# Linear attention ahead of two expert layers: the output products on 64x64 quadrants, k v in small PSUM tiles, the first k and v loaded first

## The chip, the cores and the metric

One Trainium2 chip, one of its cores. The metric is device time in microseconds (us); lower is better. Engines are named as in the profile: PE (TensorE matmul), PEld (TensorE weight load), DVE (VectorE), ACT (ScalarE), POOL (GpSimd), SP (SyncE, which issues most of the DMAs).

## What is computed

All data are fp32: q, k, v of 8 batches x 8 heads x 576 positions x 64. The change lies in the attention, the first of three stages.

```python
kv = np.einsum('bhsd,bhse->bhde', k, v)
out = np.einsum('bhsd,bhde->bhse', q, kv)
rms = np.sqrt(np.mean(out * out, axis=-1, keepdims=True) + 1e-06)
attn = out / rms * g_norm
x = attn.transpose(0, 2, 1, 3).reshape(4608, 512)
...
```

Behind it, x goes through two expert layers of 8 experts each (512 to 1024 to 512, with relu between). The first sends each token to the expert with the largest cosine logit, scaled by that expert's probability. The second gives every expert 576 tokens, by the order of all logits.

## The kernel before

**Attention (lines 267 to 351).** Each head's 64x64 matrix k v is made once and then multiplied with all of q. With the head's 64 columns go 8 more (E), the head's part of the gate logits, so a head's matrix is 64 x 72 (KW = 72). Batches are taken in pairs, four groups (gi = 0 to 3) of two batches; a group has two halves of four heads (hg). A half group is five units (u = 0 to 4): unit u is a transpose of q (`qa`, line 301: four PE transposes into a PSUM tile "tp" and one ACT copy to qT) and an output product (`qb`, line 313). Units 0 to 3 hold 2 of the 9 positions that a partition keeps, 128 rows of qT; unit 4 holds the last one, 64 rows. In all there are 40 units, 32 whole ones and 8 half ones (group 3 takes its two half units last).

`kv(m)` (line 267) makes the matrices of one batch's four heads, m = 0 to 15, in two steps. First 36 products of 64x64 by 64 columns add k v over the 9 positions in one PSUM tile (line 277), and ACT copies the result twice side by side into kvn (line 282). Two pumps later four products with `gex` (line 288) turn a head's matrix and append the gate's 8 columns; two copies of 64 partitions each (line 292, one by DVE, one by ACT) bring them to `kvx`. There each head has 2 x 72 columns: the upper 64 rows hold the matrix in the first 72, the lower 64 rows in the second 72, and the other two quarters are zero (memsets on POOL, line 261). So one product of 128 rows of qT by 144 columns gives the results of both positions, and half of its factors are zero.

`qb` makes 8 such products of 128x64 (line 333, 64 columns of output partitions for each of the two batches). Then come a copy of the 64 columns into the row tile x (line 340 or 342; DVE, or ACT where the unit's number in the group stands in EVAC, line 52), ACT's square (line 345), ACT's copy of the logits (line 347), and, one unit later on DVE, the sum of the squares (line 350).

**PSUM.** The pool has three kinds of tile with two buffers each: "mm" (two banks: output products, both steps of `kv`), "tp" (transposes) and "sm" (gate, slots and table of `group_end`). A buffer's next use waits until its last reader is done. The Tile framework also sets one engine's access to a PSUM tile behind another's.

**Order.** Every engine runs its instructions in the order of the program text. The loop of lines 894 to 929 takes the units in turn: unit n+2's transposes, unit n's output products, and then `pump()`, one step of every generator in `bg`: `kv` of the next half group (appended at units 1 and 2 of each half group; the last two at 0 and 1) and `group_end` of the group before (appended at a group's first unit). `group_end` (line 353) is norm, logits, expert choice, slots and table: some 30 small DVE instructions, some on ACT and POOL, three kinds of products on PE and the stores of x. Weight casts (`wcast`, ACT and DVE) stand at the units of CASTS, weight loads at those of LOADS.

**Loads (lines 130 to 163).** SP issues all q, k and v loads, 0.59 MB each. k and v have four buffers each, q six; load m+4 of k and v is issued when the products of m have been issued, and waits on SP's queue until these are done. The first in the queue are the expert embeddings, tau and g_norm (lines 154, 156, 158), then k and v of m = 0.

**Start (lines 851 to 878).** 44 transposes of the identity on PE; DVE's chain on the embeddings (`gate_weights`, lines 225 to 248, with one square root on ACT); the first step of kv(0) and kv(1); the gate's transposes on PE and their copies to `gex`; then the second steps of kv(0) and kv(1), and the units.

**Behind attention.** `group_end(3)` and the expert layers, from about 145 us on, fill the other 930 us. The diff touches none of it.

Of the kernel before, what the change touches and what calls it, by code (L numbers as in the profile page):

```python
# [7 lines left out]
F32 = mybir.dt.float32  # L8
# [3 lines left out]
AF = mybir.ActivationFunctionType  # L12
OP = mybir.AluOpType
AX = mybir.AxisListType
# [34 lines left out]

PEG = (4.5, 0.0)  # L50

EVAC = ((4, 8), (1, 2, 4, 5, 7, 8, 9), (1, 2, 4, 5, 7, 8, 9), tuple(range(10)))

CASTS = {25: 0, 26: 0, 28: 0, 32: 0, 34: 0, 36: 0}

# [16 lines left out]
def fused_kernel(ctx, tc, q, k, v, g_norm, emb, tau, w1, w2, wgate, v1, v2, out):  # L72
    nc = tc.nc
    V = nc.vector
    B, H, S, D = q.shape
# [18 lines left out]
    psum = pss.enter_context(tc.tile_pool(name="psum", bufs=2, space=PSUM))  # L94
# [9 lines left out]
    def mk(pool, shape, dtype, name, **kw):  # L104
        if pool is mp:
            pool = MP[name in MP0]
        return pool.tile(shape, dtype, name=name, **kw)
# [15 lines left out]
    ap = att.enter_context(tc.tile_pool(name="att", bufs=2, side="right"))  # L123
# [6 lines left out]
    def load_main(b, nm, hg):  # L130

        s = {"k": k, "v": v, "q": q}[nm]
        i = 4 * (b // 2) + 2 * hg + b % 2
        t = mk(ap, [128, 2, KR, D], F32, "qmain", bufs=6) if nm == "q" else KVL[nm, i % NL]
        nc.sync.dma_start(t.rearrange("p h r d -> p h (r d)"),
                          src(s, (b * H + 4 * hg) * S * D, [[KR * D, 128], [2 * S * D, 2], [1, KR * D]]))
        LD[nm, b, hg] = t


    def load_kv(m):  # L140
        for nm in "kv":
            load_main(m // 4 * 2 + m % 2, nm, m // 2 % 2)

    def load_q(ph):
        for j in range(2):
            load_main(ph // 2 * 2 + j, "q", ph % 2)
# [3 lines left out]
    for i in range(NL):  # L150
        for nm in "kv":
            KVL[nm, i] = mk(kvp, [128, 2, KR, D], F32, f"{nm}main{i}")
    em = mk(gp, [128, 1, XP], F32, "xt", bufs=2)[:E, 0, :HD]
    nc.sync.dma_start(em, emb)
    tau8 = con([E, 1], F32, "tau8")
# [1 line left out]
    gB = con([128, D], F32, "gB")  # L157
    nc.sync.dma_start(gB, src(g_norm, 0, [[0, 128], [1, D]]))
    for m in range(4):
        load_kv(m)  # L160
        if m % 2:
            load_q(m // 2)

# [87 lines left out]
    KW = D + E  # L251
# [4 lines left out]
    V.memset(run, 0.0)  # L256
    NKV = 4

    kvx = [mk(ap, [128, 2, 4, 2, KW], F32, f"kvx{i}", bufs=1) for i in range(NKV)]
    for t in kvx:  # L260
        nc.gpsimd.memset(t, 0.0)

    def kvh(b, h):
        hg, a, s = h // 4, h // 2 % 2, h % 2
        return kvx[b % NKV][:, a ^ s, 2 * s + hg]

    def kv(m):

        b, hg = m // 4 * 2 + m % 2, m // 2 % 2
        kvn = mk(ap, [128, 2, 2, D], F32, "kvn", bufs=2)  # L270
        p = mk(psum, [128, 2, 512], F32, "mm")
        kt, vt = LD["k", b, hg], LD["v", b, hg]
        for r in range(KR):
            for s in range(2):
                for a in range(2):
                    c = s ^ a
                    nc.tensor.matmul(p[64 * c:64 * c + 64, s, :D],
                                     vt[64 * s:64 * s + 64, a, r, :], kt[64 * s:64 * s + 64, a, r, :],
                                     start=(r == 0), stop=(r == KR - 1))
        if m + NL < 2 * B:  # L280
            load_kv(m + NL)
        nc.scalar.copy(kvn, p[:, :, None, :D].to_broadcast([128, 2, 2, D]))
        yield
        yield
        p = mk(psum, [128, 2, 512], F32, "mm")
        for s in range(2):
            for c in range(2):
                nc.tensor.matmul(p[:, c, s * KW:(s + 1) * KW], kvn[64 * c:64 * c + 64, s].rearrange("p u d -> p (u d)"),
                                 gex[64 * c:64 * c + 64, s, hg], start=True, stop=True)
        x = kvx[b % NKV]  # L290
        for r in range(2):
            (nc.scalar.copy if r else V.tensor_copy)(x[64 * r:64 * r + 64, :, hg:4:2, r],
                p[64 * r:64 * r + 64, :, :2 * KW].rearrange("p c (i w) -> p c i w", w=KW))
        yield

    GS = {}
# [16 lines left out]
    def qb(gi, u, hg, late, i):  # L313
        if u == 0 and hg == 0:
            GS[gi] = dict(s1=mk(gp, [128, TG * H], F32, "s1", bufs=2), lp=mk(gp, [128, TG * H, E], F32, "lp", bufs=2))
        if hg == 0:
            GS[gi]["x", u] = mk(gp, [128, 2, XP], F32, "xo", bufs=8) if u < 4 else mk(gp, [128, 1, XP], F32, "xt", bufs=2)
        G = GS[gi]
        qT = QT.pop((gi, u, hg))
        po = mk(psum, [128, 2, 512], F32, "mm")  # L320
        n = 8 if u < 4 else 4
        if u < 4:
            ov = po[:, :, :4 * KW].rearrange("p a (h r w) -> p a h r w", h=2, r=2)
        else:
            ov = po[:, :, :2 * KW].rearrange("p a (c w) -> p a c w", w=KW)
        for a in range(2):
            for s in range(2):
                for j in range(2):
                    kv_ = kvh(2 * gi + j, 4 * hg + 2 * a + s)
                    qt = qT[:, 2 * j + a, 64 * s:64 * s + 64]  # L330
                    if u == 4:
                        kv_, qt = kv_[:64, 0], qt[:64]
                    nc.tensor.matmul(ov[64 * j:64 * j + 64, a, s], qt, kv_, start=True, stop=True)  # L333
        o3 = po[:, :, :n // 2 * KW].rearrange("p a (c w) -> p a c w", w=KW)
        sq = mk(ap, [128, 8, D], F32, "sq")
        x = G["x", u]
        c0 = u * 16 + hg * n
        cp = nc.scalar.copy if i in EVAC[gi] else V.tensor_copy
        if u < 4:
            cp(x[:, :, hg * 4 * D:(hg + 1) * 4 * D].rearrange("p r (a c d) -> p a c r d", a=2, c=2), ov[:, :, :, :, 0:D])  # L340
        else:
            cp(x[:, 0, hg * 4 * D:(hg + 1) * 4 * D].rearrange("p (a c d) -> p a c d", a=2, c=2), ov[:, :, :, 0:D])
        if late is not None:
            late()
        nc.scalar.activation(sq[:, :n].rearrange("p (a c) d -> p a c d", a=2), o3[:, :, :, 0:D], AF.Square)

        nc.scalar.copy(G["lp"][:, c0:c0 + n].rearrange("p (a c) n -> p a c n", a=2), o3[:, :, :, D:KW])  # L347

        def later():
            V.tensor_reduce(G["s1"][:, c0:c0 + n], sq[:, :n], axis=AX.X, op=OP.add)  # L350
        return later

    def group_end(gi):
# [458 lines left out]
    def logits_w(e, c):  # L812
        N = WID[0, e][c]
        i = e - (E - ND)
        parts = [H7[0][:, :, 256 * c:256 * c + N]] if e == E - 1 else [h.bitcast(F32)[:, :, :N] for h in HT[0, e, c]]
        pl = mk(psum, [128, 512], F32, "sm")
        for kf in range(KF):
            g = kf % 4
            for x, p in enumerate(parts):
                nc.tensor.matmul(pl[32 * g:32 * g + 32, :N], W2G[0][:, i, kf - g:kf - g + 4, :].rearrange("p k e -> p (k e)"),  # L820
                                 p[:, kf, :], start=(kf < 4 and x == 0), stop=(kf >= 4 and x == len(parts) - 1),
                                 tile_position=(0, 32 * g))
        lgT = mk(mp, [128, C1 - 256], F32, "lgT")
        nc.scalar.copy(lgT[:, :N], pl[:, :N])
        return lambda: rows_l(e, c, lgT, 40)
# [45 lines left out]

    bg = []
    kv0, kv1 = kv(0), kv(1)
    next(kv0)
    next(kv1)
# [18 lines left out]
    for n, st in enumerate(steps):  # L894
        gi, u, hg = st
        i = n % 10
        ph, l = divmod(n, 5)
        l -= KVAT if ph + 2 < 2 * NG else 0
        if ph + 1 < 2 * NG and 0 <= l < 2:
            bg.append(kv(2 * ph + 2 + l))  # L900
        if n + 2 < len(steps):
            qa(*steps[n + 2])
        if n % 5 == 3 and ph + 3 < 2 * NG:
            load_q(ph + 3)
        late = qb(*st, late, i)
        if i == 0 and gi > 0:
            bg.append(group_end(gi - 1))
# [502 lines left out]
    a = logits_w(e6, 0)  # L1410
    xtiles(0, e7, 2, 3)
    a()
    b = logits_w(e6, 1)
# [77 lines left out]
    a = logits_w(e7, 1)  # L1491
# [232 lines left out]
    for e in range(1, E):  # L1724
        for g in range(2):
            for i in range(2):
                f = 2 * i + g
# [397 lines left out]
```

## Time and profile before

| | us |
|---|---|
| median of 3 runs (1075.4 to 1078.71) | 1076.03 |
| the profiled execution, its own time | 1077.35 |
| its span | 1075.6 |
| PE busy, share of the span | 1027.9, 96% |
| DVE, ACT, POOL busy | 727.3, 529.7, 298.1 |
| attention: first to last output product | 21.2 to 137.1 |

The span runs from the first to the last instruction on the device. Durations below are of the one profiled execution. "Idle before, releaser" is an engine's idle time ahead of an instruction and the instruction that ended it. A matmul's rows count records: one fp32 product is two matmul records and two weight loads, and a row of the timeline merges neighbours of the same kind.

### The profile page before, as it was taken

The numbers are of one execution on the slowest core, as the hardware profiler recorded it, in microseconds if no ns is written. First come the engines' busy times: TensorE is split into PE (matmuls) and PEld (weight loads), VectorE is DVE, ScalarE is ACT, GpSimd is POOL, SyncE is SP. The second block draws the span as 40 slices with busy tenths as digits, with TensorE's granted clock in tenths as the row PEclk, the third lists the DMA queues.
The fourth block names the chain that finished last, engine by engine and source line by source line (L and its number), as shares of the span: only waits on it lengthen the run. The fifth ranks groups of instructions, "written<-read, shape, count | busy, mean of one in ns | idle before, by whom it ended". The sixth has DMA issues, their size and how long they took to land. (4 is left out here: it accounts for less than half of the span.)

```text
span 1075.6 us, 21056 instructions
## 1 busy us (share of the span) xinstructions
PE 1027.9 (96%) x8497; PEld 937.0 (87%) x8497; DVE 727.3 (68%) x1440; ACT 529.7 (49%) x921; POOL 298.1 (28%) x396
## 2 busy tenths in 40 slices
PE   8998769899999999999999998999999999999998
PEld 7776669889999999999988987989889898989896
DVE  4466585376977778786756765677685959595860
ACT  2566633564444435363543322456565656555551
POOL 2022428261616051432400112222314131313211
PEclk8999989999999999999999999999999999999999
DMA  8999364544343535343311114435344343434311
GB/s 318 347 342 336 101 221 148 168 142 139 118 133 107 159 96 163 97 153 112 124 60 53 48 37 125 155 104 163 129 135 146 109 159 118 148 98 150 106 55 44
DMA packets 86040, 152.37 MB, mean 142 GB/s; under 512 B 6998, under 2 KB 39766, under 8 KB 85938
## 3 DMA queue, kind: packets, MB, share of 16 engines
q1 hardware_dynamic: 74450, 114.35, 32.5%
q0 software_dynamic: 10960, 36.10, 10.2%
q8 instruction: 67, 1.10, 0.4%
q10 hardware_dynamic: 528, 0.52, 0.2%
q14 instruction: 35, 0.29, 0.1%
HBM read 121.14 MB, written 29.82 MB: 140 GB/s over the span
## 5 line engine op out<-in xcount | busy, mean ns | idle before, releaser
L666 PE MATMUL mm<-xh,whi 128*128 128x256 f32 (+8 forms) x512 | 155.6, 304 | 9.8 <-ACT xh L636 6.6
L711 PE MATMUL mm<-hh,whi 128*128 128x256 f32 (+8 forms) x512 | 156.9, 306 | 1.5 <-ACT hh L683 1.5
L712 PE MATMUL mm<-hl,whi 128*128 128x256 f32 (+8 forms) x512 | 152.5, 298 | 1.1 <-DVE hl L1474 0.6
L667 PE MATMUL mm<-xl,whi 128*128 128x256 f32 (+8 forms) x512 | 152.8, 298 | 0.3 <-DVE xl L637 0.3
L668 PE MATMUL mm<-xh,wlo 128*128 128x256 f32 (+8 forms) x512 | 152.8, 298 | 0.0
L713 PE MATMUL mm<-hh,wlo 128*128 128x256 f32 (+8 forms) x512 | 152.2, 297 | 0.0
L808 DVE SCALAR_TENSOR_TENSOR rc<-xg,big 128x512 bf16<-128x512 f32 x128 | 111.1, 868 | 2.6
L666 PEld LDWEIGHTS mm<-xh,whi 128*128 128x128 f32 x512 | 97.9, 191 | 11.5 <-ACT xh L636 6.8
L548 DVE TENSOR_TENSOR wlo<-wraw,whi 128x1024 fp32r<-128x1024 f32 x72 | 90.8, 1263 | 24.4 <-ACT whi L542 23.9
L711 PEld LDWEIGHTS mm<-hh,whi 128*128 128x128 f32 x512 | 97.5, 190 | 3.5 <-ACT hh L683 1.8
L712 PEld LDWEIGHTS mm<-hl,whi 128*128 128x128 f32 x512 | 97.6, 191 | 1.5 <-DVE hl L1474 0.8
L667 PEld LDWEIGHTS mm<-xl,whi 128*128 128x128 f32 x512 | 97.8, 191 | 0.5 <-DVE xl L637 0.5
L668 PEld LDWEIGHTS mm<-xh,wlo 128*128 128x128 f32 x512 | 97.8, 191 | 0.0
L713 PEld LDWEIGHTS mm<-hh,wlo 128*128 128x128 f32 x512 | 97.4, 190 | 0.0
L720 ACT COPY yT<-mm 128x512 f32<-128x512 f32 (+8 forms) x31 | 19.9, 643 | 156.7 <-PE mm L713 156.7
L615 POOL DMA_INDIRECT xg<-xbuf,tabi x40 | 42.9, 1072 | 168.6 <-ACT sj L574 93.9
L2024 POOL DMA_INDIRECT out<-tm,ti x40 | 40.6, 1016 | 163.2 <-ACT tm L2022 143.6
L542 ACT CAST whi<-wraw 128x1024 fp32r<-128x1024 f32 x72 | 74.8, 1042 | 0.1
L683 ACT ACTIVATE hh<-mm 128x512 fp32r<-128x512 f32 (+7 forms) x56 | 36.8, 658 | 73.5 <-PE mm L668 70.2
L1767 DVE TENSOR_TENSOR wlo<-wraw,whi 128x1024 fp32r<-128x1024 f32 (+1 forms) x63 | 61.0, 986 | 11.6 <-ACT whi L1770 11.6
L333 PE MATMUL mm<-kvx,qT 128*64 128x144 f32 (+1 forms) x640 | 51.6, 297 | 12.1 <-ACT lp L347 6.4
L2034 POOL DMA_INDIRECT xg<-ybuf,tab x40 | 44.7, 1116 | 61.0 <-SPq L1559 25.6
(354 smaller groups left out, 2692.2 us busy)
## 6 DMA issues: line engine op xcount, KB each, us to landing
wraw<-in_moe_w SPq DMA_DIRECT2D x127, 512.0 KB, 3.5
kmain<-in_k SPq DMA_DIRECT2D x16, 576.0 KB, 6.6
vmain<-in_v SPq DMA_DIRECT2D x16, 576.0 KB, 13.5
qmain<-in_q SPq DMA_DIRECT2D x16, 576.0 KB, 12.0
ybuf<-yr SPq DMA_DIRECT2D x32, 260.0 KB, 2.2
xbuf<-xo POOLq DMA_DIRECT2D x12, 528.0 KB, 9.4
xg<-in_moe_w SPq DMA_DIRECT2D x16, 256.0 KB, 3.7
xbuf<-xo SPq DMA_DIRECT2D x4, 528.0 KB, 2.8
```

The source lines that it names most:

```text
L333: nc.tensor.matmul(ov[64 * j:64 * j + 64, a, s], qt, kv_, start=True, stop=True)
L542: nc.scalar.copy(hi, raw)
L548: eng.tensor_tensor(lo, raw, hi.bitcast(F32), op=OP.subtract)
L666: nc.tensor.matmul(o, a, xh[:, kd, :N], start=(kd == 0), stop=False)
L667: nc.tensor.matmul(o, a, xl[:, kd, :N], start=False, stop=False)
L668: nc.tensor.matmul(o, b, xh[:, kd, :N], start=False, stop=(kd == KD - 1))
L711: nc.tensor.matmul(o, a, hh[:, kf, :N], start=(kf == 0), stop=False)
L712: nc.tensor.matmul(o, a, hl[:, kf, :N], start=False, stop=False)
L713: nc.tensor.matmul(o, b, hh[:, kf, :N], start=False, stop=(kf == KF - 1))
L808: V.scalar_tensor_tensor(junk, raws[i], 1.0, wgB[:, x], op0=OP.mult, op1=OP.mult, accum_out=w2g[:, i // KF, i % KF, x:x + 1])
L1767: V.tensor_tensor(l, x, h.bitcast(F32), op=OP.subtract)
L2034: nc.gpsimd.indirect_dma_start(out=xg[:n, :YP], out_offset=None, in_=ybuf[:, :], in_offset=bass.IndirectOffsetOnAxis(ap=tab2[:n, e * SC + ...
```

## The change

The output products of a whole unit become 16 of 64x64 by 72 columns, each with the rows of one position (r) and the columns of one batch (j); the positions lie in separate PSUM banks. Half units keep their 8 products in another order. `kvx` loses its zero quarters and their memsets: all 128 rows hold each head's matrix, twice. The tiles of `kv` move from "mm" to "sm", two small tiles for each step, and their copies are cut by tile. The copies by ACT and DVE are handed out anew (EVAC). The loads of k and v of m = 0 are issued ahead of the embeddings, tau and g_norm.

```diff
--- before.py
+++ after.py
@@ -49,7 +49,7 @@
 
 PEG = (4.5, 0.0)
 
-EVAC = ((4, 8), (1, 2, 4, 5, 7, 8, 9), (1, 2, 4, 5, 7, 8, 9), tuple(range(10)))
+EVAC = ((4, 8), (1, 3, 5, 7, 9), (1, 3, 5, 7, 9), (1, 2, 3, 5, 6, 7, 8, 9))
 
 CASTS = {25: 0, 26: 0, 28: 0, 32: 0, 34: 0, 36: 0}
 
@@ -150,6 +150,7 @@
     for i in range(NL):
         for nm in "kv":
             KVL[nm, i] = mk(kvp, [128, 2, KR, D], F32, f"{nm}main{i}")
+    load_kv(0)
     em = mk(gp, [128, 1, XP], F32, "xt", bufs=2)[:E, 0, :HD]
     nc.sync.dma_start(em, emb)
     tau8 = con([E, 1], F32, "tau8")
@@ -157,7 +158,8 @@
     gB = con([128, D], F32, "gB")
     nc.sync.dma_start(gB, src(g_norm, 0, [[0, 128], [1, D]]))
     for m in range(4):
-        load_kv(m)
+        if m:
+            load_kv(m)
         if m % 2:
             load_q(m // 2)
 
@@ -256,9 +258,7 @@
     V.memset(run, 0.0)
     NKV = 4
 
-    kvx = [mk(ap, [128, 2, 4, 2, KW], F32, f"kvx{i}", bufs=1) for i in range(NKV)]
-    for t in kvx:
-        nc.gpsimd.memset(t, 0.0)
+    kvx = [mk(ap, [128, 2, 4, KW], F32, f"kvx{i}", bufs=1) for i in range(NKV)]
 
     def kvh(b, h):
         hg, a, s = h // 4, h // 2 % 2, h % 2
@@ -268,29 +268,29 @@
 
         b, hg = m // 4 * 2 + m % 2, m // 2 % 2
         kvn = mk(ap, [128, 2, 2, D], F32, "kvn", bufs=2)
-        p = mk(psum, [128, 2, 512], F32, "mm")
+        p = [mk(psum, [128, D], F32, "sm") for _ in range(2)]
         kt, vt = LD["k", b, hg], LD["v", b, hg]
         for r in range(KR):
             for s in range(2):
                 for a in range(2):
                     c = s ^ a
-                    nc.tensor.matmul(p[64 * c:64 * c + 64, s, :D],
+                    nc.tensor.matmul(p[s][64 * c:64 * c + 64],
                                      vt[64 * s:64 * s + 64, a, r, :], kt[64 * s:64 * s + 64, a, r, :],
                                      start=(r == 0), stop=(r == KR - 1))
         if m + NL < 2 * B:
             load_kv(m + NL)
-        nc.scalar.copy(kvn, p[:, :, None, :D].to_broadcast([128, 2, 2, D]))
-        yield
-        yield
-        p = mk(psum, [128, 2, 512], F32, "mm")
+        for s in range(2):
+            nc.scalar.copy(kvn[:, s], p[s][:, None, :].to_broadcast([128, 2, D]))
+        yield
+        yield
+        x = kvx[b % NKV]
+        p = [mk(psum, [128, 2, KW], F32, "sm") for _ in range(2)]
         for s in range(2):
             for c in range(2):
-                nc.tensor.matmul(p[:, c, s * KW:(s + 1) * KW], kvn[64 * c:64 * c + 64, s].rearrange("p u d -> p (u d)"),
+                nc.tensor.matmul(p[c][:, s], kvn[64 * c:64 * c + 64, s].rearrange("p u d -> p (u d)"),
                                  gex[64 * c:64 * c + 64, s, hg], start=True, stop=True)
-        x = kvx[b % NKV]
-        for r in range(2):
-            (nc.scalar.copy if r else V.tensor_copy)(x[64 * r:64 * r + 64, :, hg:4:2, r],
-                p[64 * r:64 * r + 64, :, :2 * KW].rearrange("p c (i w) -> p c i w", w=KW))
+        for c in range(2):
+            (nc.scalar.copy if c else V.tensor_copy)(x[:, c, hg:4:2], p[c])
         yield
 
     GS = {}
@@ -318,36 +318,28 @@
         G = GS[gi]
         qT = QT.pop((gi, u, hg))
         po = mk(psum, [128, 2, 512], F32, "mm")
-        n = 8 if u < 4 else 4
-        if u < 4:
-            ov = po[:, :, :4 * KW].rearrange("p a (h r w) -> p a h r w", h=2, r=2)
-        else:
-            ov = po[:, :, :2 * KW].rearrange("p a (c w) -> p a c w", w=KW)
-        for a in range(2):
-            for s in range(2):
-                for j in range(2):
-                    kv_ = kvh(2 * gi + j, 4 * hg + 2 * a + s)
-                    qt = qT[:, 2 * j + a, 64 * s:64 * s + 64]
-                    if u == 4:
-                        kv_, qt = kv_[:64, 0], qt[:64]
-                    nc.tensor.matmul(ov[64 * j:64 * j + 64, a, s], qt, kv_, start=True, stop=True)
-        o3 = po[:, :, :n // 2 * KW].rearrange("p a (c w) -> p a c w", w=KW)
+        m = 2 if u < 4 else 1
+        n = 4 * m
+        ov = po[:, :m, :4 * KW].rearrange("p r (c w) -> p r c w", w=KW)
+        for c in range(4):
+            for j in range(2):
+                for r in range(m):
+                    nc.tensor.matmul(ov[64 * j:64 * j + 64, r, c],
+                                     qT[64 * r:64 * r + 64, 2 * j + c // 2, c % 2 * 64:c % 2 * 64 + 64],
+                                     kvh(2 * gi + j, 4 * hg + c)[64 * r:64 * r + 64], start=True, stop=True)
         sq = mk(ap, [128, 8, D], F32, "sq")
         x = G["x", u]
         c0 = u * 16 + hg * n
         cp = nc.scalar.copy if i in EVAC[gi] else V.tensor_copy
-        if u < 4:
-            cp(x[:, :, hg * 4 * D:(hg + 1) * 4 * D].rearrange("p r (a c d) -> p a c r d", a=2, c=2), ov[:, :, :, :, 0:D])
-        else:
-            cp(x[:, 0, hg * 4 * D:(hg + 1) * 4 * D].rearrange("p (a c d) -> p a c d", a=2, c=2), ov[:, :, :, 0:D])
+        cp(x[:, :, hg * 4 * D:(hg + 1) * 4 * D].rearrange("p r (c d) -> p r c d", c=4), ov[:, :, :, 0:D])
         if late is not None:
             late()
-        nc.scalar.activation(sq[:, :n].rearrange("p (a c) d -> p a c d", a=2), o3[:, :, :, 0:D], AF.Square)
-
-        nc.scalar.copy(G["lp"][:, c0:c0 + n].rearrange("p (a c) n -> p a c n", a=2), o3[:, :, :, D:KW])
+        sqv = sq[:, :n].rearrange("p (r c) d -> p r c d", r=m)
+        nc.scalar.activation(sqv, ov[:, :, :, 0:D], AF.Square)
+        nc.scalar.copy(G["lp"][:, c0:c0 + n].rearrange("p (c r) n -> p r c n", r=m), ov[:, :, :, D:KW])
 
         def later():
-            V.tensor_reduce(G["s1"][:, c0:c0 + n], sq[:, :n], axis=AX.X, op=OP.add)
+            V.tensor_reduce(G["s1"][:, c0:c0 + n].rearrange("p (c r) -> p r c", r=m), sqv, axis=AX.X, op=OP.add)
         return later
 
     def group_end(gi):
```

## Rows read from the trace of the kernel before

**Rows 1.** Windows: length, then busy us (instructions) by engine, PEclk, DMA share, GB/s.

```profile
21.21:48.30 27.09, 25.84 (x522) 20.99 (x521) 12.23 (x21) 15.53 (x40) 0.00 (x0) 0.94 1.06 386
48.30:76.82 28.52, 26.80 (x523) 21.68 (x522) 17.73 (x44) 17.60 (x45) 5.76 (x17) 0.92 0.89 309
76.82:108.06 31.24, 26.62 (x532) 21.27 (x531) 20.46 (x47) 20.71 (x49) 5.53 (x17) 0.95 0.93 333
108.06:137.08 29.02, 21.26 (x360) 16.87 (x361) 17.70 (x44) 19.06 (x45) 12.29 (x20) 0.94 0.41 129
137.08:144.66 7.58, 1.02 (x8) 0.78 (x8) 6.82 (x15) 2.76 (x10) 2.67 (x7) 0.59 0.39 154
144.66:1075.60 930.94, 910.32 (x6333) 840.55 (x6333) 642.56 (x1219) 449.88 (x726) 265.87 (x316) 0.99 0.38 120
```

**Rows 2.** Timeline of PE in group 0: start us, us, instructions, idle before.

```profile
24.62 1.28 PE L277 MATMUL mm<-kmain,vmain 64*64 64x64 f32 x72
25.83 0.63 PE L309 MATMUL tp<-ident,qmain 128*64 128x128 f32 x4
26.39 1.20 PE L333 MATMUL mm<-kvx,qT 128*64 128x144 f32 x16
27.52 1.28 PE L277 MATMUL mm<-kmain,vmain 64*64 64x64 f32 x72
...
32.10 0.72 PE L333 MATMUL mm<-kvx,qT 64*64 64x72 f32 x16 [0.40 <-ACT lp L347]
32.74 0.67 PE L288 MATMUL mm<-gex,kvn 64*128 64x72 f32 x8
```

**Rows 3.** Waits, 0 to 140 us: engine, tile, releaser: us, times, longest.

```profile
ACT sq L345 <- DVE xo L340: 17.7, 13, 2.0
ACT kvx L292 <- DVE kvx L292: 11.5, 9, 3.5
```

**Rows 4.** Timeline, all engines, in group 3.

```profile
124.44 0.44 DVE L292 COPY kvx<-mm 64x288 f32<-64x288 f32 x1
...
125.36 2.18 PE L333 MATMUL mm<-kvx,qT 128*64 128x144 f32 x14 [3.45 <-ACT kvx L292]
```

**Rows 5.** Groups by form, 0 to 140 us: busy us, mean ns, idle before.

```profile
L340 ACT COPY xo<-mm 128x512 f32<-128x512 f32 x19 | 11.2, 591 | 10.2 <-PE mm L333 9.5 <-issue 0.7
...
L340 DVE COPY xo<-mm 128x512 f32<-128x512 f32 x13 | 9.0, 691 | 19.8 <-PE mm L333 19.8
...
L292 DVE COPY kvx<-mm 64x288 f32<-64x288 f32 x16 | 7.2, 447 | 9.1 <-PE mm L288 9.1
L347 ACT COPY lp<-mm 128x64 f32<-128x64 f32 x32 | 6.9, 217 | 0.0
...
L292 ACT COPY kvx<-mm 64x288 f32<-64x288 f32 x16 | 6.3, 394 | 11.7 <-DVE kvx L292 11.5
L282 ACT COPY kvn<-mm 128x256 f32<-128x256 f32 x16 | 6.1, 382 | 9.2 <-PE mm L277 9.0
```

**Rows 6.** Timeline, all engines, at the start.

```profile
0.86 0.41 SPq L154 DMA_DIRECT2D xt<-in_moe_expert_emb  x1
...
2.05 0.43 SPq L135 DMA_DIRECT2D kmain<-in_k  x1
...
5.22 0.65 DVE L228 TENSOR_TENSOR sq<-xt 8x512 f32<-8x512 f32 x1
...
8.35 0.74 DVE L236 SCALAR_TENSOR_TENSOR xt<-xt,en,gB 8x512 f32<-8x512 f32 x1
...
12.95 2.20 PE L277 MATMUL mm<-kmain,vmain 64*64 64x64 f32 x72 [1.70 <-DMA vmain<-in_v]
```

**Rows 7.** Source line 333: idle of PE ahead of it, by what ended it.

```profile
  issue: 4.3, 14
```

**Rows 8.** Timeline of PE in group 0, from 45.8 us.

```profile
45.83 0.47 PE L333 MATMUL mm<-kvx,qT 64*64 64x72 f32 x7 [0.74 <-issue]
...
48.30 1.90 PE L333 MATMUL mm<-kvx,qT 128*64 128x144 f32 x16
```

## The prediction

> **What bounds the kernel now.** I read the windows first, cut at the starts of the attention groups [rows 1]. Attention runs from 21.2 to 137.1 us; behind it lies one DVE chain of 7.6 us, and then 930.9 us in which PE is busy 98% of the time with work that the diff doesn't touch. So the change is worth what it moves the end of attention, and the rest shifts with it. In the four attention windows PE is busy 25.8 of 27.1, 26.8 of 28.5, 26.6 of 31.2 and 21.3 of 29.0 us, while DVE and ACT are at 45 to 66%. The DMA share is 1.06 in the first and 0.41 in the last. PE is thus the first bound of groups 0 to 2; in group 3 it shares that with others.
>
> Busy is not work, though, so I take start to start from PE's timeline [rows 2]. One output product of a unit of 128 columns (line 333, 8 products of 128x64 by 144 columns) holds PE for 1.13 us (26.39 to 27.52). The products of k and v (line 277, 36 products in all four quadrants) hold it for 1.21 us (24.62 to 25.83), four transposes for 0.56, and a half unit (u = 4, 8 products of 64x64 by 72 columns, in two quadrants) for 0.64 (32.10 to 32.74). Line 288's products take some 0.6 (0.67 with their tail at 32.74). Five transpose groups, four whole units, one half unit, two k v products and two of line 288 are 2.9 + 4.5 + 0.6 + 2.4 + 1.2 = 11.7 us per half group. There are eight half groups, in all 115.9 us; less 90 of such work (8 x 11.7, and the last half group has no k v) some 26 us are waits and slow clock.
>
> What the waits are: ACT's square waits for the copy of the same PSUM tile by DVE, 17.7 us over 13 times, and ACT's half of line 292 waits for DVE's half, 11.5 us over 9 [rows 3]. PE waits longest in group 3: the last products of 121.45 start again at 125.36, after 3.45 us of waiting for ACT's half of line 292, which followed DVE's half; that one started at 124.44, in a queue in which the end work of the group before stood ahead of it [rows 4]. That wait is DVE's.
>
> **The parts of the change, priced.**
>
> *Output products by quadrants.* 8 products of 144 columns become 16 of 72, on 64x64 tiles, all four quadrants in turn. No row shows this form with 72 columns. The nearest is line 277: four quadrants in turn, 72 records in 1.21 us, 16.8 ns each at 64 columns. Scaled by 72/64, 32 records take 0.60 us. Bounds: the same records at the half unit's pace (16 in 0.64, two quadrants only) give 1.28; scaling today's 1.13 by the columns streamed (72 x 4 against 144 x 4, four pairs against four fours) gives 0.57. I take 0.60, since line 277 is the same tile size and the same way round the quadrants. That is 0.53 us less for each of 32 whole units, 17.0 us of PE work. The half units are unchanged.
>
> How much of it lies on the path? In half groups 0, 1 and 3 PE is what the others wait for (DVE's copy waits 19.8 us for PE over 13 times [rows 5]): 12 units in full, 6.4 us. In half groups 2, 4 and 5 the end work of a group or weight casts stand on DVE and ACT: two thirds of 12 units, 4.2. In group 3 the first three units count, 1.6; the fourth runs into the DVE wait of 125.36 and is lost; of the last four, that wait for ACT, half, 1.1. Sum 13.3.
>
> *k v in tiles of its own.* Line 282 goes from one ACT copy of 256 elements, 382 ns, to two of 128. ACT's copies of 64 and 512 elements take 217 and 591 [rows 5], so 128 cost about 270 and the pair 540: 16 x 0.16 = 2.5 us more on ACT. Line 292's halves go from 288 elements on 64 partitions to 144 on 128, about 290 ns on DVE (from 447; slope from 447 at 288 and 691 at 512) and 284 on ACT (from 394), and they no longer follow one another, since each has its own tile. The first output product of a half group needs both halves: in turn they take 0.84 us, against 0.56 of transposes that PE has in between, side by side 0.29, which the transposes cover. So 0.28 us in each of seven half groups: 2.0 us gained. The ring of two big tiles is then left to the output products alone, and the ring of two small ones carries k v, the gate's transposes and the slots: line 277 of a next step waits for both ACT copies of the one before. Between them lie a transpose group and an output product, 0.56 + 0.60 us, and ACT's copy, square and small copy before them. I cost that at nothing while DVE is prompt; where DVE is late it falls in the wait that I counted as lost.
>
> *Copies moved by EVAC.* Groups 1 and 2 give DVE one whole and one half copy each, group 3 two whole: 4 x 0.69 + 2 x 0.41 (256 elements on the same slope) = 3.6 us more on DVE, against 16 x 0.16 = 2.5 less in line 292. Net 1.1 us, and about 1.0 of it on the path, since DVE sets the end in part of groups 1 to 3. ACT is relieved of four copies of 0.59, two half ones and 1.8 us in line 292, against the 2.5 above.
>
> *First loads ahead.* k and v of step 0 go out at 0.86 instead of 2.05 us [rows 6], 1.2 us earlier, and so do all big loads behind them as long as DMA is full (share 1.06). PE waits for v at 12.95, so that product comes up to 1.2 us earlier. Against that, three small loads fall behind 1.2 MB; at the 386 GB/s of the first attention window this is 3 us, so the embeddings land near 9 instead of before 5.2. The DVE chain on them ran from 5.22 to 9.09; begun near 9 it ends at 13, and PE wants it after the second k v product, near 13.9. That is covered by 0.9 us, and the rest would be paid from there. The small ring also makes the first steps' gate transposes and line 288's products take turns: two copies of 0.27 and 0.29 us come between, with their hand-overs some 0.9 us. Start: -0.3, between -1.2 and +1.5.
>
> *The zero halves.* Four memsets on POOL at the start, that nobody waits for: nothing, as POOL's next result is wanted by DVE only after its chain on the embeddings, which ends at 9.09 [rows 6].
>
> *More instructions.* 512 matmul records more. Line 333's 640 cost 4.3 us in 14 waits that the profile calls issue [rows 7]. In proportion 3.4 us, at the least nothing; I take 1.7.
>
> **Sum:** -13.3 - 2.0 - 0.3 + 1.0 + 1.7 = -12.9 us. The profiled execution took 1077.35 us (span 1075.6), 1.3 above the median of 1076.03. So 1064.4 for that execution, and 1063.1 from the median.
>
> **The rivals.**
>
> *Evacuation takes PE's place.* PE needs 9.8 us per half group; DVE and ACT are already busy some 8.9 to 10.4 in groups 1 to 3 [rows 1], and each unit's copy, square and small copy are one chain of 0.69 + 0.59 + 0.22 on two engines. If the waits grow by what PE saves from group 1 on, only group 0 counts: 8 x 0.53 = 4.2, with 2.0 and 0.3, less 2.7: about -4, 1072. [...] Against it: both engines still have a third of their time free in groups 1 and 2 [rows 1], and the kv tiles no longer stand in the big ring. Chance 0.18.
>
> *The clock falls more often (slower).* After a wait of 0.74 us at 45.83 the next whole unit of line 333 (48.30) took 1.90 us instead of 1.20 [rows 8], and after the wait of 125.36 2.18 [rows 4]. [...] A PE with a fifth less work waits more. [...] For it: each fall stands behind a wait of about 0.7 us or more. Against it: most such waits are DVE's, they stay, and no new ones of that length arise in groups 0 and 1. Chance 0.05.
>
> *The quadrants don't overlap.* Then a unit costs 1.28, 0.15 more: +4.8 - 2.0 - 0.3 + 1.0 + 1.7 = +5, 1081. Line 277 speaks plainly against it. Chance 0.03.
>
> *All of it lands.* 17.0 of PE work and 3 us more of waits on the shared ring: -22, 1054 to 1057. DMA does not forbid it: its share is 0.93 and less from group 1 on [rows 1]. Chance 0.12.
>
> **The numbers.** The forecast has 0.62, from 1058 to 1068 by its terms (units lost between a third and none, issue 0 to 3.4, start -1.2 to +1.5). The range for 8 in 10 reaches up to the evacuation case, 1072, and down to 1056. A measurement of this kernel can tell about 0.3%, 3.2 us. Faster: forecast, full gain and two thirds of the evacuation case, 0.86; within 0.3%: 0.08; slower: 0.06.
>
> **What would show it.** Line 333's group start to start at 0.55 to 0.65 us, its records doubled to 1152; the two copies of line 292 side by side; ACT's wait for DVE there gone; attention ending near 124; the stretch behind it as long as now. A start to start near 1.2, a PEclk under 0.85 in the attention windows, or PE's waits grown by over 10 us would make it wrong; so would a wait for q, k or v after 30 us, or PE waiting for line 248 at the start.

## The result: slower by half a per cent

The changed kernel took 1083.86 us (median of 6 runs, 1080.38 to 1087.28) against 1078.56 of the kernel before (6 runs, 1075.4 to 1078.9). The ratio is 1.0056 [1.0033, 1.0079]: slower, by more than the 0.3% that can be told from no change. The prediction had 1063.1 us, 1056 to 1072, and gave slower 0.06. The profiled execution is the longest of the six, 1087.28 us (span 1085.5), so the two profiles differ by 9.9 us of span where the medians differ by 5.3.

The windows of the profile after, cut as those of before [rows 1] (length, busy us of each engine with its instructions, PEclk, DMA share, GB/s); the first is the start:

```profile
8.12:22.64 14.52, 10.21 (x182) 8.79 (x181) 4.26 (x23) 2.60 (x8) 0.00 (x0) 0.63 1.03 382
22.64:52.19 29.55, 25.11 (x650) 20.93 (x649) 11.43 (x21) 14.27 (x42) 0.00 (x0) 0.78 0.93 336
52.19:83.33 31.14, 25.16 (x652) 20.90 (x651) 17.89 (x47) 17.03 (x51) 5.79 (x17) 0.84 0.87 307
83.33:113.64 30.31, 25.08 (x632) 20.89 (x632) 19.45 (x47) 17.15 (x46) 3.61 (x15) 0.78 0.86 313
113.64:145.86 32.22, 23.97 (x517) 19.79 (x517) 21.76 (x48) 19.57 (x51) 14.22 (x23) 0.71 0.40 132
145.86:153.40 7.54, 2.37 (x9) 1.78 (x9) 6.78 (x15) 2.46 (x9) 2.67 (x7) 0.50 0.38 152
153.40:1085.50 932.10, 909.77 (x6333) 840.44 (x6332) 642.16 (x1218) 448.95 (x725) 264.24 (x316) 0.99 0.37 119
```

The last two stretches are nearly as long as before (7.54 and 932.1 against 7.58 and 930.9). The loss lies in attention and its start. PEclk is 0.71 to 0.84 there, where before had 0.92 to 0.95. From the first output product to the last, before and after (same columns):

```profile
21.21:136.86 115.65, 100.30 (x1933) 80.66 (x1932) 67.90 (x155) 72.67 (x178) 23.57 (x54) 0.94 0.82 288
```

```profile
22.64:145.54 122.90, 99.00 (x2445) 82.33 (x2444) 70.21 (x162) 67.87 (x187) 23.62 (x54) 0.78 0.76 269
```

This pair holds most of the 9.9 us. PE was to lose 17.0 us of work; its busy time fell by 1.3. Its idle time rose from 15.35 to 23.90. Together that is 7.25 us more, and the first product starts 1.4 later.

PE's timeline of group 0 (start, us, instructions, idle before and what ended it), which answers to [rows 2]:

```profile
26.81 0.63 PE L309 MATMUL tp<-ident,qmain 128*64 128x128 f32 x4
27.37 0.73 PE L327 MATMUL mm<-kvx,qT 64*64 64x72 f32 x32
27.92 1.23 PE L277 MATMUL sm<-kmain,vmain 64*64 64x64 f32 x72
29.08 0.55 PE L309 MATMUL tp<-ident,qmain 128*128 128x128 f32 x3
32.31 0.48 PE L309 MATMUL tp<-ident,qmain 128*128 128x128 f32 x1 [2.69 <-issue]
32.72 1.24 PE L327 MATMUL mm<-kvx,qT 64*64 64x72 f32 x32
33.89 1.13 PE L290 MATMUL sm<-gex,kvn 64*128 64x72 f32 x8
34.95 1.11 PE L309 MATMUL tp<-ident,qmain 128*128 128x128 f32 x4
35.99 1.23 PE L327 MATMUL mm<-kvx,qT 64*64 64x72 f32 x16
...
41.47 1.20 PE L327 MATMUL mm<-kvx,qT 64*64 64x72 f32 x32
42.48 1.23 PE L277 MATMUL sm<-kmain,vmain 64*64 64x64 f32 x72
```

The product of a unit (line 327, was 333) takes 0.55 us start to start (27.37 to 27.92), as priced. Then PE stops for 2.69 us in the middle of four transposes, and waits for no engine, tile or load that the profile shows: "issue". Behind the stop PE's work takes about twice as long: the next unit 1.17 us (32.72 to 33.89), four transposes 1.04 (34.95 to 35.99) instead of 0.56. The granted clock was 0.50 of full speed from 32.3 to 42.5 us, the lower of the two levels in its records (1.00 and 0.50).

PE's waits, 22 to 146 us (us, times, longest), and the line of line 327's page that answers to [rows 7]:

```profile
PE mm L327 <- issue: 8.4, 4, 3.0
PE mm L327 <- DVE kvx L293: 4.4, 1, 4.4
PE mm L327 <- ACT lp L339: 3.8, 2, 2.5
PE sm L290 <- DVE kvx L293: 2.9, 2, 2.0
PE tp L309 <- issue: 2.7, 1, 2.7
PE sm L277 <- issue: 1.6, 3, 1.2
```

```profile
  issue: 24.7, 38
```

"issue" ahead of line 333 was 4.3 us in 14 waits [rows 7]; it is 24.7 in 38 ahead of line 327. Both sums add the idle time of the weight loads (PEld) to that of PE, and [rows 7] calls all of it PE's. For PE alone it was 0.7 us in one wait before, and it is 8.4 in four now.

What the stops are shows in the DMA view of 26.4 to 29.8 us and, in the second fence, of 29.8 to 31.0 (queue, kind: packets, MB, share of 16 engines):

```profile
q1 hardware_dynamic: 612, 1.33, 105.4%
```

```profile
q1 hardware_dynamic: 207, 0.45, 99.9%
q8 instruction: 1, 0.02, 5.9%
```

PE's own program comes through the DMA engines too, on queue q8, in packets of 16,384 bytes. In the records one packet goes with each 256 PE instructions (18150 records of PE and PEld to 72 packets, 17155 to 67 before), and the stops lie where a run of 256 ends. PE passed such an end at 26.42 us; the loads on q1 had all 16 engines (105.4%), and the next packet ran only from 29.83 to 30.96. PE started the last instruction of its run, the 256th behind the end at 26.42, at 29.35 and went on at 32.31. So this run lasted 2.93 us; in the kernel before the runs of group 0 lasted 5.6 to 6.8. With the DMA engines quiet (share 0.18 from 118 to 125 us), at 119 and 123 us, a packet started 0.4 and 0.7 us after PE passed the end. PE ran dry one run behind the end that it had passed: at 26.42 it had no more than one packet's 256 instructions ahead.

Up to the last output product PE's instruction records rose from 4374 to 5369. I count as a stop each step of over 0.3 us from one instruction's start to the next at the end of such a run: four before, 3.1 us; eight after, 14.3 us. Behind each of the eight PE went on 1.2 to 1.5 us after the end of a packet.

### The profile page after: what moved, and what is told of

Read it like the earlier page. It is cut to its first block, busy times and chain, and to the rows that moved or that the text cites. A ratio compares the mean times of both kernels' runs of the same rounds, so it can differ in the third digit from the quotient of the medians.

```text
span 1085.5 us, 22067 instructions
## 1 busy us (share of the span) xinstructions
PE 1028.3 (95%) x9009; PEld 940.0 (87%) x9009; DVE 727.6 (67%) x1446; ACT 523.5 (48%) x931; POOL 292.2 (27%) x392
## 5 line engine op out<-in xcount | busy, mean ns | idle before, releaser
L601 POOL TENSOR_TENSOR xg<-xg,gB 128x512 f32<-128x512 f32 (+7 forms) x37 | 60.6, 1639 | 2.9
```

The lines of the kernel that those rows point to most:

```text
L601: eng.tensor_tensor(x, x, gB[:n, None, :].to_broadcast([n, H, D]), op=OP.mult)
```

## The experiments

Ratios are against the kernel before on the same chip. Stops, low clock and lengths of stretches are those of one profiled execution each. "Stops" are counted as above, "low" is the time at 0.50 of the full clock between the first and the last output product.

**Quadrants alone.**

```diff
-    kvx = [mk(ap, [128, 2, 4, 2, KW], F32, f"kvx{i}", bufs=1) for i in range(NKV)]
-    for t in kvx:
-        nc.gpsimd.memset(t, 0.0)
+    kvx = [mk(ap, [128, 2, 4, KW], F32, f"kvx{i}", bufs=1) for i in range(NKV)]
...
+        for c in range(2):
+            (nc.scalar.copy if c else V.tensor_copy)(x[:, c, hg:4:2], p[:, c, :2 * KW].rearrange("p (i w) -> p i w", w=KW))
```

and line 333's products as in the change.

> The kernel before with the quadrant products alone (and the copies of line 292 cut by 128 rows instead of 64, as their layout needs). Theory fetch (PE reads its instructions in blocks of 16 KB by DMA; twice the records of line 333 make it run dry while q, k and v fill the DMA engines, and the clock falls behind each such stop): slower than before by 3 to 9 us, four to eight stops of PE over 1 us put down to issue, PEclk 0.75 to 0.88 in the attention windows. Theory rest (the small ring, EVAC and the load order cost the time, the products gain): faster than before by 6 us or more.

Measured: 1077.47 us, 1.0023 [1.0008, 1.0038]; stops 19.2 us, low 39.8 us, 120.80 us from first to last product. The part that was to bring 13.3 us loses some 2.5 by the ratio (1.9 between the medians), a little less than the expected 3 to 9, with more stops than the whole change has. The 120.80 us are one execution, the fastest of its twelve (1075.40).

**The load order alone, and all but the quadrants.** The first edit is `load_kv(0)` ahead of the small loads. The second takes also the new EVAC and the small tiles for k v, with line 333 as before.

> The kernel before with k and v of step 0 loaded ahead of the three small loads, and nothing else. If the order of the loads is a loss, as the first output product at 22.64 instead of 21.21 us in the changed kernel may say: +1 to +1.5 us. If the small ring makes that loss: within 0.5 us of before, with the second k v product near 13.0 as before, since its load goes out no earlier.

> The kernel before with all but the quadrant products and the layout of kvx: k v sums in two small tiles with two ACT copies, EVAC and load order as changed; line 292 stays in the big tile. Theory fetch: within 2 us of before on either side (1076 to 1081), stops put down to issue as few as before (3 to 4 us in all). Theory rest: slower by 4 us or more.

Measured: 1073.79 us, 0.9987 [0.9969, 1.0006], stops 2.6, low 7.6; and 1079.65 us, 1.0039 [1.0021, 1.0056], stops 3.6, low 18.7. The load order costs nothing that can be told. With the new EVAC and the small tiles it costs 4 us without new stops, where the prediction had a gain; the expectation of no loss without stops was missed.

**Without the loads.** Three kernels end behind attention, and 36 of the 48 q, k and v loads are left out (each reads the tile of an earlier load): the changed kernel, the kernel before, and quadrants alone.

```diff
+        if nm != "q" and i >= NL:
+            LD[nm, b, hg] = KVL[nm, i % NL]
+            return
```

> The changed kernel cut off behind attention, and without 36 of the 48 loads of q, k and v: from m = 4 on the products read the buffers that hold the first ones, so DMA has little to do behind some 25 us. Both expert stages are left out and the attention of later batches is that of the first. Theory fetch: PE's stops over 0.6 us put down to issue between 30 us and the end of attention vanish (under 1 us in all, against some 14), PEclk over 0.92, and the last output product ends near 120 us instead of 146. Theory form (the clock falls because of the products on quadrants themselves): no such stops, yet PEclk stays at 0.7 to 0.85. If the stops are no matter of DMA they stay as they are.

> The kernel before, ended behind attention and with 36 of the 48 q, k and v loads left out: the counterpart of the changed kernel so cut (108.0 us from the first output product to the last). Only that stretch is read. Theory fetch (PE stops for instructions that stand behind the loads, and the clock falls behind the stops): before had 3.1 us of stops and 14.8 us of low clock, so without loads it shortens by 2 to 4 only, to 111 to 114 us, and the changed kernel is then the shorter one by 3 to 6. Theory form (the new attention is itself no shorter, whatever the loads do): 106 to 109 us, as long as the changed one.

> Products by quadrants alone on the kernel before, ended behind attention, the same 36 loads left out. With loads this form took 120.8 us from first output product to last, with 19.2 us of stops at block ends and 39.8 us of low clock. Theory fetch: stops under 8 us, low clock under 20 us, the stretch 101 to 106 us, shorter than before without loads by over 6. Theory form: stops gone but the stretch within 3 us of before without loads.

Windows from first to last output product, of the kernel before, of quadrants alone and of the changed kernel, all without these loads:

```profile
19.38:133.97 114.59, 101.97 (x1932) 82.53 (x1932) 67.92 (x155) 72.86 (x179) 23.54 (x54) 0.90 0.35 123
```

```profile
17.58:124.97 107.39, 86.23 (x2445) 70.57 (x2444) 66.07 (x153) 68.95 (x177) 23.09 (x54) 0.89 0.38 130
```

```profile
21.85:129.86 108.01, 86.89 (x2445) 72.32 (x2444) 69.27 (x161) 66.26 (x186) 23.55 (x54) 0.88 0.34 118
```

Without the loads quadrants shorten attention, from 114.59 to 107.39 us; with them they lengthen it, from 115.65 to 120.80. Each length is one execution: with the loads, three kernels with the old products, EVAC and tiles took 113.2, 115.6 and 117.3 us, and three with quadrants in their place 118.6, 118.9 and 120.8. PE's busy time falls by 15.7 us without the loads, near the 17.0 priced. So the form is sound, and with the loads its gain is lost. Stops: none in the kernel before, 11.2 us with quadrants alone, 8.1 in the changed kernel. The low clock is 22.4, 23.1 and 26.1 us. So the theory's numbers were missed in all three: stops under 1 us and PEclk over 0.92 in the changed kernel (8.1, 0.88), 111 to 114 us for the kernel before, and stops under 8, low clock under 20 and 101 to 106 us for quadrants alone. Some of these stops (4.7 of the 11.2, 3.3 of the 8.1) fall before 32 us, while the loads that are left still fill the DMA engines. Others remain where these are nearly idle: quadrants alone passed an end at 64.46 us and the next at 67.80, 3.3 us later; with the DMA share at 0.04 the packet started 1.5 us behind the first end, took 0.9, and PE went on 1.5 us behind it, at 68.35. PE's waits in quadrants alone:

```profile
PE tp L312 <- issue: 5.9, 3, 3.2
PE mm L330 <- ACT lp L342: 5.1, 7, 1.8
PE mm L330 <- DVE kvx L296: 3.9, 2, 3.3
PE mm L281 <- issue: 2.0, 3, 1.0
PE mm L292 <- ACT kvx L296: 1.8, 2, 0.9
PE mm L330 <- issue: 1.4, 2, 0.8
PE mm L281 <- ACT lp L342: 0.7, 2, 0.4
```

Waits for ACT and DVE are 11.5 us here and 12.1 in the kernel before without loads (5.1 for lp, 4.7 and 2.3 for kvx): with the old EVAC, evacuation did not take PE's place. What is new is 9.3 us of issue.

**Releasing the loads one by one.** Quadrants alone, with each later load held back until a unit is through:

```diff
+        if sq is not None:
+            nc.gpsimd.tensor_copy(t[:1, 0, 0, :1], sq[:1, 0, :1])
```

> Products by quadrants alone (as in the first run: 1077.47 us, 19.2 us of stops at block ends, 39.8 us of low clock in attention), and the q, k and v loads behind the first fourteen released one in each unit, two where more than two stand ready: GpSimd writes one element of the load's tile after the unit's sq, so that SP can't start the load before. Without loads this form had 11.2 us of stops and took 107.4 us from the first output product to the last. Theory fetch: fewer loads stand ahead of each packet of instructions, so stops of 9 to 13 us, low clock under 30 us, and 1068 to 1073 us. Rival (the stops don't depend on how many loads stand in the queues, or the loads come late instead): stops as before or PE waits for a DMA of q, k or v; 1076 us or more.

Measured: 1078.71 us, 1.0033 [1.001, 1.0057]; stops 16.7, low 38.1. The expectation of a gain was missed, and the run says nothing on the queues' depth: from 60 to 84 us a q load still took 9.6 us from issue to landing (10.1 without the edit), so the edit did not shorten what stands ahead of a packet. The DMA share from 22 to 113 us is still 0.88 to 0.97. So the one test of how many loads stand ahead of a packet decided nothing; that packets come late where loads fill the DMA engines is shown (up to 4.1 us behind the end of a run in the changed kernel, 0.4 and 0.7 with the DMA engines quiet), whether they stand behind queued loads or are held by something else is not.

**EVAC.** Undone in the changed kernel, and alone beside the load order:

```diff
-EVAC = ((4, 8), (1, 2, 4, 5, 7, 8, 9), (1, 2, 4, 5, 7, 8, 9), tuple(range(10)))
+EVAC = ((4, 8), (1, 3, 5, 7, 9), (1, 3, 5, 7, 9), (1, 2, 3, 5, 6, 7, 8, 9))
```

> The changed kernel with one edit undone: the share of the output tiles that ACT evacuates is that of before (table EVAC), all else as changed. The two halves of the change cost +2.5 us (products alone) and +4 us (the rest alone). Theory share (the new EVAC moves copies to VectorE, which then comes late to the k v copies): the part that costs +4 is gone, so 1077 to 1079 us, and PE's waits for VectorE's kvx copy (4.4 us in group 3) fall under 3.5. Theory ring (the k v sums in small tiles cost the +4): within 2 us of the changed kernel, 1082 to 1085. By both, PE's stops at the ends of instruction blocks stay (10 to 20 us of issue in the group of the output products).

> The kernel before with the first loads moved ahead and the new EVAC; products, k v sums and their PSUM tiles as before. Theory share: as slow as the rest of the change alone, 1078 to 1081 us (ratio 1.003 to 1.005), with PE waiting for k v copies by over 2 us in places. Theory ring: as the load order alone, 1073 to 1075.5 (ratio under 1.000).

Measured: undone 1080.68 us, 1.0064 [1.0043, 1.0085], by the ratio as slow as the whole change, so the theory of the share missed (the 4.4 us wait in group 3 stays too); alone 1080.14 us, 1.0053 [1.0036, 1.007], against 0.9987 of the load order alone. With the old products the new EVAC thus costs some 7 us, give or take 3. Its stops are 3.0 us, as few as those of the load order alone (2.6), yet its low clock is 31.7 us against 7.6: at 61.73 us line 290's products took 1.13 us, behind 1.68 us of waiting for ACT's kvx copy, and at 57.21 0.67. PE's waits for kvx grew from 7.0 to 9.5 us, its busy time from 97.9 to 105.2. Timelines near 55 us, of the load order alone and, in the second fence, with the new EVAC:

```profile
54.27 0.59 ACT L342 COPY xo<-mm 128x512 f32<-128x512 f32 x1 [0.56 <-PE mm L335]
...
54.68 0.76 DVE L388 TENSOR_TENSOR lp<-lp,r 128x576 f32<-128x576 f32 x1
...
59.68 0.44 DVE L294 COPY kvx<-mm 64x288 f32<-64x288 f32 x1
```

```profile
54.40 0.69 DVE L342 COPY xo<-mm 128x512 f32<-128x512 f32 x1 [2.93 <-PE mm L335]
...
57.03 0.76 DVE L388 TENSOR_TENSOR lp<-lp,r 128x576 f32<-128x576 f32 x1
...
60.81 0.44 DVE L294 COPY kvx<-mm 64x288 f32<-64x288 f32 x1
61.73 1.13 PE L290 MATMUL mm<-gex,kvn 64*128 64x72 f32 x8 [1.68 <-ACT kvx L294]
```

One output copy went from ACT to DVE. Its 0.69 us are not the price: DVE stands idle 2.93 us until PE has made that tile, and the end work of the group before (line 388) and the kvx copy stand behind it on DVE. Line 388 moves from 54.68 to 57.03, and PE waits for kvx. This is one place of several; no row divides the 7 us among them.

**First loads with quadrants; small tiles undone in the changed kernel.**

> Products by quadrants and the first loads ahead, on the kernel before; k v sums and EVAC as before. Quadrants alone cost +2.5 us, with loads and small tiles (old EVAC) +6.9. Theory start (the load order takes the early start back: the first product comes early, PE stands idle until the second load, the gate weights come late): first output product at 20.5 to 22.5 instead of 18.12, 1079 to 1082 us. Rival ring (the small tiles cost the difference): first output product under 19.5 and 1076 to 1078 us.

> The changed kernel with the k v sums back in halves of the big PSUM tiles; quadrant products, first loads and the new EVAC stay. With the old EVAC the small tiles made 1.0064 [1.0043, 1.0085] out of 1.0029 [1.0004, 1.0054]. Theory ring (beside quadrants the two small tiles cost some 3.5 us: the copies of one k v step stand ahead of the next, at the start and where DVE is late): ratio 1.001 to 1.004, 1076 to 1079 us, and PE's waits for DVE's kvx ahead of line 290's products (2.9 us in the changed kernel) gone. Rival share (with quadrants, as alone, the new EVAC costs the time, and the tiles nothing): 1.005 to 1.008, 1080 to 1084 us.

Measured: 1077.21 us, 1.0029 [1.0004, 1.0054], first product at 20.81, the start of the one expectation and the time of the other; and 1080.42 us, 1.0048 [1.0029, 1.0067], between the two expectations. With quadrants, EVAC undone (1.0064), tiles undone (1.0048) and nothing undone (1.0056) cannot be told apart; with both undone 1.0029 is left, and the intervals overlap. How the 3 us between divide stays open. The stops divide the kernels more clearly: the six with quadrants throughout and all loads have 14.3 to 19.2 us of them and 37.6 to 54.6 of low clock, the five with the old products 2.6 to 3.6 and 7.6 to 31.7 (the 31.7 with the new EVAC).

**The zeros.**

```diff
-        nc.gpsimd.memset(t, 0.0)
...
+    for t in kvx:
+        nc.scalar.copy(t.rearrange("p x a b c -> p (x a b c)"), zt.to_broadcast([128, 16 * (D + E)]))
```

> The kernel before, with one edit: the zeros of the kvx tiles written by ACT behind the first step of the gate weights, not by GpSimd ahead of it (4.39 us there, while VectorE's casts took 1.13 us instead of 0.49). Theory start: the gate weights come 1.5 us earlier, the clock is not lowered at 12.2, the first output product stands at 18 to 18.7 instead of 21.21, and the time is 1072 to 1074 us. Rival (the second k v load sets the start): first output product at 20 or later, 1075 us.

Measured: 1073.89 us, 0.9987 [0.9957, 1.0016], first product at 21.31. The theory fell: the memsets set nothing, as the prediction had it. Whether the 18.12 of quadrants alone is an effect of the edit stays open: the same form without the later loads began at 17.58, its paced kernel, also without memsets, at 21.52. In quadrants alone PE's second k v product took 1.28 us (at 12.74), in the kernel before 2.20 (at 12.95), where the clock was lowered from 12.2 us on for 10.2 us; in the paced kernel the granted clock was 0.64 from 8 to 22 us.

**Quadrants where DMA is quiet.** Load order, and the new products for the last group alone:

```diff
-        late = qb(*st, late, i)
+        late = (qb3 if gi == NG - 1 else qb)(*st, late, i)
```

with `qb3` the new products, and kvx of batches 6 and 7 copied without zero halves.

> The kernel before with the first loads ahead (ratio 0.9987 [0.9969, 1.0006] by itself, 1073.8 us) and products by quadrants in the last group of ten units alone, behind some 113 us, where the DMA engines are busy 0.4 of the time and a packet of instructions starts within 1 us. Theory fetch: no more stops there than the 2.6 us of the load order alone (up to 4), PE's work in the group shortened by up to 10 x 0.53 = 5.3 us, of which 1 to 4 reach the end because VectorE's chain has its share there: 1069.5 to 1073 us. Rival (VectorE and ACT set this group): PE waits longer for the kvx copy and for lp, 1073 to 1075.5 us.

Measured: 1071.62 us (12 runs), 0.9976 [0.9953, 0.9998]: 0.2% under the kernel before, at the edge of what can be told, and not to be told from the load order alone (0.9987). Stops 3.3 us and low 7.3 up to the last group; over all of attention 4.3 and 14.1. PE at two points of the last group, in this kernel and, in the second fence, in the load order alone:

```profile
121.27 1.29 PE L372 MATMUL mm<-kvx,qT 64*64 64x72 f32 x28 [3.31 <-DVE kvx L295]
...
132.24 1.40 PE L670 MATMUL tp<-ident,xg 128*128 128x128 f32 x8
```

```profile
121.66 2.18 PE L335 MATMUL mm<-kvx,qT 128*64 128x144 f32 x14 [3.44 <-ACT kvx L294]
...
134.53 1.93 PE L635 MATMUL tp<-ident,xg 128*128 128x128 f32 x8
```

From the wait for kvx, which stays, to the first work behind attention it is 10.97 us instead of 12.87. In these rows the form gains where it stands; over the whole kernel that gain is not shown.

## Why the prediction was wrong, point by point

**More instructions, +1.7 (0 to 3.4): the step that failed.** I scaled the "issue" of [rows 7] with the number of records, and took its 4.3 us as PE's, while 3.5 of them are the weight loads' and one wait of 0.7 is PE's. In the rows it is not a cost per record but a delivery: a run of 256 instructions has to last until the next packet is there, and PE went on 1.2 to 1.5 us behind a packet's end in each of the eight stops. The old products were slow enough for that (3.1 us of stops in 17 runs), the new ones are not, so the stops grew to 14.3 us. The rows of before held the hint: the wait at 45.83 is "issue", 0.74 us long, in the middle of a product [rows 8]. I read it as a trigger for the clock and did not ask what it was. The upper bound of 3.4 was wrong as well, since the row it came from holds the slower products alone.

**The clock, a rival at 0.05.** That the clock falls more often held: there were 54.6 us at the lower level, 14.8 before, and PEclk, 0.78 over attention, lies under the 0.85 that the text named as a sign against the forecast. The waits behind it were not those that the rival had. The step that failed is "no new ones of that length arise in groups 0 and 1". The falls in the changed kernel are granted at 32.3, 52.7, 66.4, 80.0, 97.1, 110.8, 131.2 and 141.5 us; four stand behind or in issue stops of 1.74 to 3.02 us, the others behind or in waits for kvx and lp of 0.95 to 4.40. Of the 17.0 us of work that were to be saved 15.7 came back in PE's busy time. That the stops cause those falls rests on the order of the rows, and on the kernels without loads, where in the changed kernel stops and low clock shrink together (14.3 to 8.1 and 54.6 to 26.1 us). They are not its only cause: the kernel before without loads has no stop and 22.4 us of low clock, and the new EVAC with the old products 3.0 of stops and 31.7 of low clock, some of it behind a wait for a copy (1.68 us, at 61.73). No run changed the clock alone, so how much of the loss is the clock's stays open.

**Output products, -13.3.** The unit was right: 0.60 forecast, 0.55 to 0.66 measured. The 13.3 on the path did not come. Without the loads it was 7.2, with 9.3 us of "issue" waits that were not there before; with them the end came later.

**EVAC, +1.0.** Right in sign, too small: some 7 us with the old products. I costed the copies' 3.6 us on DVE, not that DVE waits for PE's tile with the group's end work behind it.

**k v tiles, -2.0.** The copies were priced well: 0.30 us for each of line 293's halves (0.29 and 0.28 forecast), 0.43 to 0.45 for line 283's two (0.54 forecast). ACT's half no longer waits for DVE's; these are ACT's waits in the changed kernel, 0 to 150 us, which answer to [rows 3]:

```profile
ACT sq L338 <- DVE xo L334: 26.4, 17, 5.9
...
ACT kvx L293 <- PE sm L290: 5.2, 6, 2.7
```

No run shows the gain: with the old products the small tiles made 1.0039 out of 1.0053, within the intervals; in group 3 PE waits 4.40 us for DVE's copy, which starts at 132.44 in a queue, against 3.45 [rows 4].

**Start, -0.3 (-1.2 to +1.5).** +1.4 in the profiled execution, inside the bounds. k v of step 0 came first, but PE's second product began at 13.05, as before at 12.95 [rows 6]: its load went out behind the small ones. Line 290 then took 3.35 us instead of 2.42, in turns with the small tiles' copies. The first output product stood between 18 and 23 us in all full kernels, so this term is barely larger than that scatter.

**Evacuation takes PE's place, 0.18.** Not seen: without the loads PE's waits for ACT and DVE were 11.5 us with quadrants and 12.1 with the old products; with the loads they were 11.1 in the changed kernel and 12.6 in the one before. Nor did the rival of quadrants that don't overlap come true: 0.55 us a unit, not 1.28.

## What to carry to other kernels

Smaller matmuls cost instructions, and PE's instructions are data: here line 333's 640 records became 1152, each 256 PE instructions came in a DMA packet of 16,384 bytes, and the stops at the ends of runs grew from 3.1 to 14.3 us. Where loads fill the DMA engines (share 0.86 to 0.93 in groups 0 to 2) and PE has little slack, count the PE instructions per microsecond, look for PE's "issue" idle and for the instruction queue in the DMA view, and try the short form where DMA is quiet (share 0.48 from 110 to 135 us, in the run with the new products in the last group alone: 10.97 us instead of 12.87 there). A copy moved to another engine can cost the time for which that engine then waits for it (2.93 us for a copy of 0.69), with all that stands behind, not its duration alone. When a cut in PE's work meets new waits, compare PE's busy time before and after: it shows at once what came back (15.7 of 17.0 us here, with PEclk at 0.78 instead of 0.94).

## What was not expected of the hardware

A packet of instructions took 0.9 to 1.3 us in attention of the changed kernel, and after a stop PE went on 1.2 to 1.5 us behind its end (30.96 to 32.31). The share of the instruction queue is 1% of the DMA time in attention, and still 14.3 us of stops end behind its packets. From first to last output product, before and after:

```profile
q8 instruction: 15, 0.25, 0.8%
```

```profile
q8 instruction: 19, 0.31, 1.0%
```

Four packets more went with 11 us more of stops. While the loads were thick a packet started up to 4.1 us after PE passed the end of a run in the changed kernel, and up to 6.5 in the one before (85.62 to 92.14, DMA share 1.03), where the run lasted 10.6 us and PE did not stop. Where the DMA engines stood idle, in the kernels without loads, it started 0.3 to 1.7 us after.
